# Three joined edits: half rows' pv over 128 keys, slot exponentials transposed in whole blocks, five rows' copies on ScalarE

## The chip, the cores and the metric
The kernel runs on one core of a Trainium2 chip. A core has a TensorE (PE), a VectorE (DVE), a ScalarE (ACT), a GpSimd (POOL) and a SyncE (SP) that issues most DMAs. Each engine works through its own queue in order, and semaphores tie the queues together. The metric is device time in microseconds; a median of three runs stands for a kernel.

## The reference
Three stages follow each other, all in float32 at the outside:

```python
# 4 batches, 8 heads, 576 positions, head dimension 64
scores = q @ k.T / sqrt(64)                       # per head
cum = cumsum(log(clip(f, 1e-4, 1)))
scores = where(causal, -1e9, scores + cum[:, None] - cum[None, :])
x = softmax(scores) @ v                           # -> 2304 tokens x 512

h = x @ w_in                                      # 512 x 2048
x = (h * sigmoid(1.702 * h)) @ w_out              # 2048 x 512

logits = x @ phi                                  # 32 slots, 8 experts x 4
d = softmax(logits, over tokens)                  # slot_input = d.T @ x
slot_out[e] = relu(slot_input[e] @ w1[e]) @ w2[e]
out = softmax(logits, over slots) @ slot_out
```

## The kernel before
A batch has 576 positions, so it falls into four query rows of 128 positions and one of 64. There are 20 such rows r, and each holds all 8 heads. Row 4, 9, 14 and 19 are the half rows. float32 products are made from pairs of f16 values, a high part and the rest.

`prep_row(r)` readies one row. k and q arrive by DMA as f32 (kf and qf; for rows 0 to 2 one tile kqf). ScalarE writes their f16 high parts (L318 kbn, L321 qbn). VectorE copies these into two more tiles (L322 kan, L328 qan), adds three columns of the decay sums (L323, from cpart), and subtracts to get the low parts (L325, L329; GpSimd does this in rows 1 to 4). kan, kbn, qan and qbn are single tiles, used again for every row. They are then transposed: by TensorE and a copy out of PSUM in rows 0 to 2 (L340, L342, L344), by a DMA afterwards (L346).

Rows 0 to 4 find the maximum of each query before the exponentials: score products (L382) and a reduction on VectorE (L387), then L432, a transpose mT (L436) and a ScalarE write into qa (L445), after which the real scores can be made (L467, L469) and the exponential taken (L489). From row 5 on the maximum comes with the score itself (L551, L552, L574), the probabilities are written in two f16 parts (L586, L587) and a DMA transposes them (ph<-pn, L591).

`emit_pv(r, h)` multiplies the probabilities with v, one key block j of 128 positions after another. In rows 5 to 19 each block takes three matmuls, high by high, high by low, low by high (L628 to L630). A half row's last block has 64 keys, and there the operands are sliced to 64 rows. The v tile `vv` has 128 rows; for a half row only 64 of them are filled. The probabilities of a half row's last block are padded with zeros to 128 before the DMA transposes them (L585).

The second stage is `moe_steps`: h = x @ w_in (L800 to L802), the gate (L813, L814), transposes gT (L756) and the product with phi folded into w_out (L778). Its weights arrive as f32 words and are unpacked in the first 165 us by ScalarE, VectorE and GpSimd (L208 to L216, L277, L278; L243 to L269 fold phi). `slot_steps` follows each pair of token blocks: logits lT, the exponential dT over 128 rows (the 32 slots four times), its transposes d (L896), a copy dd (L898), and the slot sums sp (L921).

The order on each engine is made by a scheduler that lays out the recorded instructions by a time model; attention steps and second-stage steps are recorded interleaved, by costs in `attn_items`. The expert weights of the third stage are loaded into tiles that attention leaves, once it has ended.

Of the kernel before, what the change touches and what calls it, by code (L numbers as in the profile page):

```python
# [14 lines left out]
AF = mybir.ActivationFunctionType  # L15
# [15 lines left out]
def attention_moe_softmoe(ctx, tc, q, k, v, f, w_in, w_out, phi, w1, w2, out):  # L31
    nc = tc.nc
    P_PV, P_XT, P_MG, P_W, P_MG2 = (1.2, 2.4, 3000, 5, 8000)
    B, H, S, D = q.shape
    NT, DM = out.shape
    DFF = w_in.shape[1]
    NS = phi.shape[1]
# [21 lines left out]
    kan, kbn, qan, qbn = [ap_.tile([128, H, 128], F16, name=n) for n in ("kan", "kbn", "qan", "qbn")]  # L59
# [14 lines left out]
    ident = const.tile([128, 128], F32, name="ident")  # L74
# [8 lines left out]
    cpart = ap_.tile([128, NQ, BH, 3], F16, name="cpart")  # L83
# [203 lines left out]
    KA, KB, QA, QB, VV = {}, {}, {}, {}, {}  # L287
# [25 lines left out]
    def prep_row(r):  # L313
        b, i = rows[r]
        n = rows_of[i]
        kf, qf = nat.pop((r, "kf")), nat.pop((r, "qf"))
        vf = nat.pop((r, "vf"), None)
        first = nc.scalar.activation(out=kbn[0:n, :, 0:D], in_=kf[0:n], func=AF.Copy)  # L318
        if r == 0:
            tc.keep_in_program_order(first)  # L320
        nc.scalar.activation(out=qbn[0:n, :, D:2 * D], in_=qf[0:n], func=AF.Copy)  # L321
        nc.vector.tensor_copy(kan[0:n, :, 0:D], kbn[0:n, :, 0:D])  # L322
        nc.vector.tensor_copy(kan[0:n, :, D:D + 3], cpart[0:n, i, b * H:(b + 1) * H, :])  # L323
        eng = nc.gpsimd if 1 <= r < 5 else nc.vector
        eng.tensor_tensor(  # L325
            out=kbn[0:n, :, D:2 * D], in0=kf[0:n], in1=kbn[0:n, :, 0:D], op=ALU.subtract
        )
        nc.vector.tensor_copy(qan[0:n, :, 0:D], qbn[0:n, :, D:2 * D])  # L328
        eng.tensor_tensor(  # L329
            out=qbn[0:n, :, 0:D], in0=qf[0:n], in1=qbn[0:n, :, D:2 * D], op=ALU.subtract  # L330
        )
        kab = ap_.tile([128, 2, H, 128], F16, tag=f"kab{r % 6}", name="kab")
        order = ((kan, KA, 0), (qan, QA, "qa"), (kbn, KB, 1), (qbn, QB, "qb"))
        for src, dst, nm in order[::-1] if r < 3 else order:
            t = kab[:, nm] if nm in (0, 1) else ap_.tile([128, H, 128], F16, tag=nm, name=nm, bufs=2)
            if r < 3:

                pt = ps.tile([128, H, 128], F16, tag="mm", name="kqT", bufs=3)
                for h in range(H):
                    nc.tensor.transpose(pt[:, h, 0:n], src[0:n, h, :], ident16[0:n, 0:n])  # L340
                if (nm in (0, 1)) == False:
                    nc.scalar.copy(out=t[:, :, 0:n], in_=pt[:, :, 0:n])  # L342
                else:
                    nc.vector.tensor_copy(t[:, :, 0:n], pt[:, :, 0:n])  # L344
            else:
                nc.sync.dma_start_transpose(  # L346
                    out=t[:, :, 0:n], in_=src[0:n].rearrange("p h c -> p (h c)")
                )
            dst[r] = t
        if b not in B32:  # L350
            vv = ap_.tile([128, 2, H, D + 1], F16, tag="vv", name="vv", bufs=6)
            nc.scalar.activation(out=vv[0:n, 0, :, 0:D], in_=vf[0:n], func=AF.Copy, scale=VS)
            nc.vector.scalar_tensor_tensor(
                out=vv[0:n, 1, :, 0:D], in0=vf[0:n], scalar=VS, in1=vv[0:n, 0, :, 0:D],
                op0=ALU.mult, op1=ALU.subtract,
            )
            nc.gpsimd.memset(vv[0:n, 0, :, D:D + 1], 1.0)
            nc.gpsimd.memset(vv[0:n, 1, :, D:D + 1], 0.0)
            VV[r] = vv
        if r == 0:  # L360
            load_row(0, "v")
            load_row(1, "v")
        elif r + 1 < len(rows):
            load_row(r + 1)
# [245 lines left out]
    def emit_pv(r, h):  # L610
        b, i = rows[r]
        base = ROW[b, 0]
        n = rows_of[i]
        p0 = 64 * (b % 2) if n < 128 else 0
        if h % 4 == 0:
            cur["pv"] = ps_pv("pv")
        pv = cur["pv"].rearrange("p (h c) -> p h c", h=4)
        o = pv[p0:p0 + n, h % 4, 0:D + 1]
        for j in range(i + 1):
            ph, off = PH.pop((r, h, j))  # L620
            rr = rows_of[j]
            if b in B32:
                nc.tensor.matmul(  # L623
                    o, lhsT=ph[0:rr, off:off + n], rhs=VV[base + j][0:rr, h, :], start=(j == 0), stop=(j == i)
                )
                continue
            vh, vl = VV[base + j][0:rr, 0, h, :], VV[base + j][0:rr, 1, h, :]
            nc.tensor.matmul(o, lhsT=ph[0:rr, 0, off:off + n], rhs=vh, start=(j == 0), stop=False)  # L628
            nc.tensor.matmul(o, lhsT=ph[0:rr, 0, off:off + n], rhs=vl, start=False, stop=False)  # L629
            nc.tensor.matmul(o, lhsT=ph[0:rr, 1, off:off + n], rhs=vh, start=False, stop=(j == i))  # L630
        if h % 4 == 3:
            blk = blk_of[r]
            if blk not in XB:
                XB[blk] = ap_.tile([128, DM], F32, tag="x" if n == 128 else "xs", name="x", bufs=1)
            x = XB[blk]
            rd = ap_.tile([128, 4, 1], F32, tag="rd", name="rd", bufs=2)
            nc.vector.tensor_scalar(
                out=rd[p0:p0 + n], in0=pv[p0:p0 + n, :, D:D + 1], scalar1=1e-9 * PB / (VS if b in B32 else 1.0), scalar2=None, op0=ALU.add
            )
            nc.vector.reciprocal(out=rd[p0:p0 + n], in_=rd[p0:p0 + n])  # L640
            g = (h // 4) * 4 * D
            nc.vector.tensor_tensor(
                out=x[p0:p0 + n, g:g + 4 * D].rearrange("p (h d) -> p h d", h=4),
                in0=pv[p0:p0 + n, :, 0:D], in1=rd[p0:p0 + n].to_broadcast([n, 4, D]), op=ALU.mult,
            )
# [4 lines left out]
    for pair in range(B // 2):  # L650
# [4 lines left out]
        n = rows_of[-1]  # L655
# [184 lines left out]
    def slot_steps(c, ts=(0, 1)):  # L840
        fresh = c == 0
        nt = len(ts)
# [3 lines left out]
            out=l4, in0=P4.pop((c, ts[0]))[:, 0:128 * nt], scalar1=1.0 / (GS * WS), scalar2=None, op0=ALU.mult  # L846
# [32 lines left out]
        dT = mp.tile([128, 256], F32, tag="dT", name="dT", bufs=1)[:, 0:128 * nt]  # L879
# [13 lines left out]
        pd = ps_mm("d")  # L893
        with nullcontext() if end else tc.issue_after(last_hp[0].ins):
            for i in range(nt):
                nc.tensor.transpose(pd[:, NS * i:NS * (i + 1)], dT[0:NS, 128 * i:128 * (i + 1)], ident[0:NS, 0:NS])  # L896
        dd = mp.tile([128, 2 * NS], F32, tag="dd", name="dd", bufs=1)[:, 0:nt * NS]
        nc.vector.tensor_copy(dd, pd[:, 0:nt * NS])  # L898
        yield

        if end:
# [8 lines left out]
            for n, v in enumerate(halves):  # L910
                nc.vector.scalar_tensor_tensor(
                    out=spart[:, v], in0=spart[:, v], scalar=nm[:, 1:2], in1=sp[n][:, v], op0=ALU.mult, op1=ALU.add
# [151 lines left out]
    if True:  # L1064
# [26 lines left out]
        n = 0  # L1091
# [10 lines left out]
        for c in range(NCH):  # L1102
            t0, t1 = goals[c], goals[c + 1]
            NSTEP = 2 * N_UNIT
            n = 0
# [181 lines left out]
```

## Time and profile before
| | |
|---|---|
| median of 3 runs | 561.03 us (560.23 to 561.23) |
| profiled execution | 562.1 us, span of its instructions 560.4 us |
| mean granted TensorE clock | 0.973 |
| TensorE busy | 506.8 us (90%), 5387 matmuls |
| VectorE busy | 354.5 us (63%) |
| ScalarE busy | 309.2 us (55%) |
| GpSimd busy | 69.0 us (12%) |
| chain that ended last | PE 70%, DMA 12%, DVE 8%, ACT 5% |

A busy share is a mean over stages with different limits. In the 40 slices of the page TensorE stands at 3 to 6 tenths in the first four (56 us) and at 8 or 9 tenths in nearly all later ones, while GpSimd is busy only in the first nine. A matmul's duration in the profile is the time it takes from start to end; matmuls overlap, so what one costs a full TensorE is read from the starts of neighbours.

### The profile page before, as it was taken

Reading aid. Unit: us, or ns where it says so; the run is one execution under the profiler, and the core shown is the slowest. Engines: PE = TensorE matmul, PEld = TensorE weight load, DVE = VectorE, ACT = ScalarE, POOL = GpSimd, SP = SyncE. Lnnn points to the kernel's source line nnn. Section 1 sums busy time; section 2 is a strip of 40 time slices with the busy share of each in tenths; the row PEclk is TensorE's granted clock in tenths of the full one; section 3 lists DMA queues with packets and bytes.
Section 4 is the critical chain, followed back from the end, with each engine's and each line's share of the span. In section 5 each row is a group of like instructions: output and inputs, shape, how many; then the busy total and the mean of one; then the engine's idle time right before and its main releaser. Section 6 shows DMA issues by size and latency. Waiting matters only on the chain.

```text
span 560.4 us, 13652 instructions
## 1 busy us (share of the span) xinstructions
PE 506.8 (90%) x5387; PEld 317.4 (57%) x5387; DVE 354.5 (63%) x934; ACT 309.2 (55%) x604; POOL 69.0 (12%) x120
## 2 busy tenths in 40 slices
PE   3566999998989999999999799989999999899991
PEld 3455876775666555665665466546566545454431
DVE  8988969787667357577776667866764413352022
ACT  6767786786767354565666566756564233312111
POOL 4866743310000000000000000000000000000000
PEclk9879799998999999999999899999999999999997
DMA  9997674999867227996759979995544199999999
GB/s 241 275 363 173 171 126 151 262 183 190 153 130 121 58 39 146 181 182 99 130 99 151 154 139 155 208 163 104 85 78 79 37 344 369 363 341 338 379 294 284
DMA packets 229823, 105.63 MB, mean 188 GB/s; under 512 B 202592, under 2 KB 211296, under 8 KB 229760
## 3 DMA queue, kind: packets, MB, share of 16 engines
q1 hardware_dynamic: 228528, 103.59, 80.0%
q10 hardware_dynamic: 1232, 1.18, 0.7%
q8 instruction: 42, 0.69, 0.5%
q14 instruction: 21, 0.17, 0.1%
HBM read 64.63 MB, written 4.72 MB: 124 GB/s over the span
## 4 chain that ended last, share of the span: by engine, by line
PE 70%; DMA 12%; DVE 8%; ACT 5%; issue 2%; SPq 2%; ACTq 0%; DVEq 0%
PE hp L800 10%; PE hp L801 9%; PE hp L802 9%; DMA ph<-pn 6%; PE gT L756 5%; PE p L778 4%; PE pv L623 3%; PE pv L628 3%; PE l L1172 3%; PE sp L921 2%; DMA kf<-in_k_dram 2%; PE scs L551 2%; DMA we<-in_moe_w_dram 2%; PE scs L552 2%; PE pv L630 2%
## 5 line engine op out<-in xcount | busy, mean ns | idle before, releaser
L800 PE MATMUL hp<-w,xt 128*128 128x512 f16 x288 | 110.4, 383 | 0.3 <-DVE spart L928 0.3
L801 PE MATMUL hp<-w,xt 128*128 128x512 f16 x288 | 109.8, 381 | 0.0
L802 PE MATMUL hp<-w,xt 128*128 128x512 f16 x288 | 109.7, 381 | 0.0
L578 ACT ACTIVATE pf<-scs,mx 128x512 f32<-128x512 f32 (+3 forms) x108 | 57.6, 541 | 40.9 <-DVE mx L574 31.7
L814 DVE SCALAR_TENSOR_TENSOR g<-g,hp 128x512 f32<-128x512 f32 x72 | 49.2, 683 | 41.6 <-ACT g L813 40.9
L813 ACT ACTIVATE g<-hp 128x512 f32<-128x512 f32 x72 | 42.6, 591 | 51.6 <-PE hp L802 46.4
L587 DVE SCALAR_TENSOR_TENSOR pn<-pf,pn 128x512 f16<-128x512 f32 (+2 forms) x78 | 51.0, 657 | 31.0 <-ACT pn L586 30.4
L586 ACT ACTIVATE pn<-pf 128x512 f16<-128x512 f32 (+2 forms) x78 | 47.0, 606 | 26.3 <-DMA ph<-pn 25.0
L628 PE MATMUL pv<-vv,ph 128*128 128x65 f16 (+2 forms) x360 | 45.9, 199 | 7.9 <-DMA ph<-pn 7.7
L574 DVE CUSTOM_DVE_ANT_0 scs<-scs,zmq 128x128 f32<-128x128 f32 (+3 forms) x96 | 46.6, 495 | 9.1 <-PE scs L552 6.9
L802 PEld LDWEIGHTS <-xt 128*128 128x128 f16 x288 | 28.3, 98 | 33.3 <-issue 0.6
L763 ACT COPY gt<-gT 128x512 f32<-128x512 f32 x71 | 41.1, 583 | 9.7 <-PE gT L756 9.3
L628 PEld LDWEIGHTS <-ph 128*128 128x128 f16 (+2 forms) x360 | 34.4, 102 | 20.0 <-DMA ph<-pn 10.2
L629 PE MATMUL pv<-vv,ph 128*128 128x65 f16 (+2 forms) x360 | 45.3, 196 | 0.0
L756 PE MATMUL gT<-ident,g 128*128 128x128 f32 x288 | 45.1, 277 | 0.0
L630 PE MATMUL pv<-vv,ph 128*128 128x65 f16 (+2 forms) x360 | 45.1, 195 | 0.0
L800 PEld LDWEIGHTS <-xt 128*128 128x128 f16 x288 | 28.8, 100 | 27.8 <-issue 4.7
L756 PEld LDWEIGHTS gT<-ident,g 128*128 128x128 f32 x288 | 33.9, 142 | 14.4 <-issue 5.0
L801 PEld LDWEIGHTS <-xt 128*128 128x128 f16 x288 | 28.3, 98 | 22.7 <-issue 0.7
L629 PEld LDWEIGHTS <-ph 128*128 128x128 f16 (+2 forms) x360 | 34.7, 103 | 1.9 <-issue 0.2
L551 PE MATMUL scs<-kab,qa 128*128 128x128 f16 x240 | 35.2, 220 | 0.4 <-ACT pf L578 0.4
L585 POOL MEMSET pn<- 128x128 f16 x12 | 2.5, 210 | 267.3 <-DMA ph<-pn 165.8
(226 smaller groups left out, 1036.3 us busy)
## 6 DMA issues: line engine op xcount, KB each, us to landing
we<-in_moe_w_dram SPq DMA_DIRECT2D x127, 256.0 KB, 5.6
raw<-in_moe_w_in_dram SPq DMA_DIRECT2D x16, 512.0 KB, 7.3
raw<-in_moe_w_out_dram SPq DMA_DIRECT2D x16, 512.0 KB, 6.0
kf<-in_k_dram SPq DMA_DIRECT2D x13, 256.0 KB, 3.7
qf<-in_q_dram SPq DMA_DIRECT2D x13, 256.0 KB, 4.1
vf<-in_v_dram SPq DMA_DIRECT2D x12, 256.0 KB, 4.4
out_dram<-ob SPq DMA_DIRECT2D x12, 256.0 KB, 3.2
ph<-pn SPq DMA_TRANSPOSE x78, 3.3
```

The source lines that it names most:

```text
L574: nc.vector.tensor_tensor_reduce(out=o, in0=o, in1=mask, scale=-SC, scalar=3.0e38 if n == 128 else DG[r][1][:, u], op0=ALU.add, op1=ALU.mi ...
L578: nc.scalar.activation(out=pf[:, hh * nb:(hh + 1) * nb], in_=o, func=AF.Exp, bias=mx[:, hh:hh + 1], scale=-1.0)
L586: nc.scalar.activation(out=pn[:, 0, 0:w], in_=pf, func=AF.Copy, scale=PB)
L587: nc.vector.scalar_tensor_tensor(out=pn[:, 1, 0:w], in0=pf, scalar=PB, in1=pn[:, 0, 0:w], op0=ALU.mult, op1=ALU.subtract)
L628: nc.tensor.matmul(o, lhsT=ph[0:rr, 0, off:off + n], rhs=vh, start=(j == 0), stop=False)
L629: nc.tensor.matmul(o, lhsT=ph[0:rr, 0, off:off + n], rhs=vl, start=False, stop=False)
L630: nc.tensor.matmul(o, lhsT=ph[0:rr, 1, off:off + n], rhs=vh, start=False, stop=(j == i))
L756: last_turn[0] = nc.tensor.transpose((pt if a < 2 else pt2)[:, a * 128:(a + 1) * 128], g[:, a * 128:(a + 1) * 128], ident)
L800: nc.tensor.matmul(hp, lhsT=xt[:, 0, kk, ts], rhs=win(0, fg, kk), start=(kk == 0), stop=False)
L801: nc.tensor.matmul(hp, lhsT=xt[:, 0, kk, ts], rhs=win(1, fg, kk), start=False, stop=False)
L802: last_hp[0] = nc.tensor.matmul(hp, lhsT=xt[:, 1, kk, ts], rhs=win(0, fg, kk), start=False, stop=(kk == KD - 1))
L814: nc.vector.scalar_tensor_tensor(out=g, in0=g, scalar=1.0, in1=hp, op0=ALU.add, op1=ALU.mult)
```

## The change
Three edits are joined.

1. In `emit_pv` the last key block of a half row is read over all 128 rows, as the other blocks are. The empty 64 rows of the half row's v tile are filled with zeros by GpSimd in `prep_row`. This concerns rows 9, 14 and 19; row 4 takes another branch and stays.
2. In `slot_steps` a transpose of dT reads all 128 rows and writes 128 columns, where it read 32 rows and wrote 32. The copy dd picks the 32 columns of each block that are used.
3. In `prep_row`, for rows 0 to 4, the copies into kan and qan are made by ScalarE from the f32 tiles kf and qf, and the decay columns are copied by ScalarE too. Rows 5 to 19 are as before.

```diff
--- before.py
+++ after.py
@@ -319,13 +319,21 @@
         if r == 0:
             tc.keep_in_program_order(first)
         nc.scalar.activation(out=qbn[0:n, :, D:2 * D], in_=qf[0:n], func=AF.Copy)
-        nc.vector.tensor_copy(kan[0:n, :, 0:D], kbn[0:n, :, 0:D])
-        nc.vector.tensor_copy(kan[0:n, :, D:D + 3], cpart[0:n, i, b * H:(b + 1) * H, :])
+        if r < 5:
+            nc.scalar.activation(out=kan[0:n, :, 0:D], in_=kf[0:n], func=AF.Copy)
+        else:
+            nc.vector.tensor_copy(kan[0:n, :, 0:D], kbn[0:n, :, 0:D])
+        (nc.scalar.copy if r < 5 else nc.vector.tensor_copy)(
+            kan[0:n, :, D:D + 3], cpart[0:n, i, b * H:(b + 1) * H, :]
+        )
         eng = nc.gpsimd if 1 <= r < 5 else nc.vector
         eng.tensor_tensor(
             out=kbn[0:n, :, D:2 * D], in0=kf[0:n], in1=kbn[0:n, :, 0:D], op=ALU.subtract
         )
-        nc.vector.tensor_copy(qan[0:n, :, 0:D], qbn[0:n, :, D:2 * D])
+        if r < 5:
+            nc.scalar.activation(out=qan[0:n, :, 0:D], in_=qf[0:n], func=AF.Copy)
+        else:
+            nc.vector.tensor_copy(qan[0:n, :, 0:D], qbn[0:n, :, D:2 * D])
         eng.tensor_tensor(
             out=qbn[0:n, :, 0:D], in0=qf[0:n], in1=qbn[0:n, :, D:2 * D], op=ALU.subtract
         )
@@ -354,6 +362,8 @@
                 out=vv[0:n, 1, :, 0:D], in0=vf[0:n], scalar=VS, in1=vv[0:n, 0, :, 0:D],
                 op0=ALU.mult, op1=ALU.subtract,
             )
+            if n < 128:
+                nc.gpsimd.memset(vv[n:], 0.0)
             nc.gpsimd.memset(vv[0:n, 0, :, D:D + 1], 1.0)
             nc.gpsimd.memset(vv[0:n, 1, :, D:D + 1], 0.0)
             VV[r] = vv
@@ -624,7 +634,8 @@
                     o, lhsT=ph[0:rr, off:off + n], rhs=VV[base + j][0:rr, h, :], start=(j == 0), stop=(j == i)
                 )
                 continue
-            vh, vl = VV[base + j][0:rr, 0, h, :], VV[base + j][0:rr, 1, h, :]
+            rr = 128
+            vh, vl = VV[base + j][:, 0, h, :], VV[base + j][:, 1, h, :]
             nc.tensor.matmul(o, lhsT=ph[0:rr, 0, off:off + n], rhs=vh, start=(j == 0), stop=False)
             nc.tensor.matmul(o, lhsT=ph[0:rr, 0, off:off + n], rhs=vl, start=False, stop=False)
             nc.tensor.matmul(o, lhsT=ph[0:rr, 1, off:off + n], rhs=vh, start=False, stop=(j == i))
@@ -893,9 +904,11 @@
         pd = ps_mm("d")
         with nullcontext() if end else tc.issue_after(last_hp[0].ins):
             for i in range(nt):
-                nc.tensor.transpose(pd[:, NS * i:NS * (i + 1)], dT[0:NS, 128 * i:128 * (i + 1)], ident[0:NS, 0:NS])
+                nc.tensor.transpose(pd[:, 128 * i:128 * (i + 1)], dT[:, 128 * i:128 * (i + 1)], ident)
         dd = mp.tile([128, 2 * NS], F32, tag="dd", name="dd", bufs=1)[:, 0:nt * NS]
-        nc.vector.tensor_copy(dd, pd[:, 0:nt * NS])
+        nc.vector.tensor_copy(
+            dd.rearrange("p (t s) -> p t s", t=nt), pd[:, 0:128 * nt].rearrange("p (t s) -> p t s", t=nt)[:, :, 0:NS]
+        )
         yield
 
         if end:
```

The scheduler lays the instructions out anew. Line numbers in the pieces of the new order are those of the changed file: L323, L326 and L334 are the copies into kan, its decay columns and qan, L348 to L352 were L340 to L344, L397 was L387.

ScalarE at the start of the program: Ln over f (fs), the table load for Exp, row 0's high parts, row 0's first copy out of PSUM (qb), row 1's high parts. Before:

```order
L140 ACTIVATE fs<-fs 32x576
L142 ACT_TABLE_LOAD
L142 ACTIVATE cres<-fs 32x1
L318 ACTIVATE kbn<-kqf 128x8x64
L321 ACTIVATE qbn<-kqf 128x8x64
L342 COPY qb<-kqT 128x1024
L321 ACTIVATE qbn<-kqf 128x8x64
L318 ACTIVATE kbn<-kqf 128x8x64
L342 COPY qa<-kqT 128x1024
```

Now:

```order
L140 ACTIVATE fs<-fs 32x576
L323 ACTIVATE kan<-kqf 128x8x64
L142 ACT_TABLE_LOAD
L142 ACTIVATE cres<-fs 32x1
L318 ACTIVATE kbn<-kqf 128x8x64
L321 ACTIVATE qbn<-kqf 128x8x64
L334 ACTIVATE qan<-kqf 128x8x64
L350 COPY qb<-kqT 128x1024
L321 ACTIVATE qbn<-kqf 128x8x64
L326 COPY kan<-cpart 128x8x3
L318 ACTIVATE kbn<-kqf 128x8x64
L350 COPY qa<-kqT 128x1024
```

Row 0's copy into kan stands ahead of the table load, its copy into qan behind the high parts, and the decay columns between row 1's high parts.

VectorE between row 1's attention output x and row 2's maxima (mt), with row 2's copies out of PSUM (kab). Before:

```order
L642 TENSOR_TENSOR x<-pv,rd 128x256
L344 COPY kab<-kqT 128x1024
L328 COPY qan<-qbn 128x8x64
L344 COPY kab<-kqT 128x1024
L322 COPY kan<-kbn 128x8x64
L323 COPY kan<-cpart 128x8x3
L387 TENSOR_REDUCE mt_83<-scm 128x1 x5
L675 TENSOR_TENSOR xt<-xT,xt 128x4x128
```

Now:

```order
L653 TENSOR_TENSOR x<-pv,rd 128x256
L352 COPY kab<-kqT 128x1024 x2
L397 TENSOR_REDUCE mt_83<-scm 128x1 x6
L686 TENSOR_TENSOR xt<-xT,xt 128x4x128
```

Row 3's three copies are gone from between the last copy out of PSUM and the first maximum.

TensorE after row 1's maxima (mT): the first pv of row 0, then row 1's scores (scs) before, the transposes of row 2 (kqT) now. Before:

```order
L436 MATMUL mT<-ident,mt_84 104x128
L623 MATMUL pv<-vv,pf 128x65 x4
L467 LDWEIGHTS kab
L467 MATMUL scs<-qa,kab 128x128
L469 LDWEIGHTS kab
```

Now:

```order
L446 MATMUL mT<-ident,mt_84 104x128
L633 MATMUL pv<-vv,pf 128x65 x4
L348 LDWEIGHTS qbn
L348 MATMUL kqT<-ident_76,qbn 128x128
L348 LDWEIGHTS qbn
```

The transposes of qbn, kbn and qan of row 2, 24 in all, now stand ahead of row 1's scores.

## Rows read from the trace of the kernel before

**Rows 1.** Stretches: length; busy PE, PEld, DVE, ACT, POOL; PE clock, DMA share, GB/s.
```profile
0.00:60.00 60.00, 33.65 (x346) 30.51 (x347) 53.51 (x99) 41.46 (x66) 40.07 (x57) 0.88 0.93 248
340.00:450.00 110.00, 107.50 (x1191) 64.89 (x1189) 71.74 (x211) 62.49 (x127) 1.28 (x12) 1.00 0.65 115
```

**Rows 2.** TensorE's waits: for whom, us in total, times, longest.
```profile
PE pv L628 <- DMA ph<-pn: 7.7, 9, 2.0
PE mT L436 <- DVE mt L432: 7.5, 2, 6.9
PE scs L467 <- DVE mt L387: 6.9, 2, 5.5
```

**Rows 3.** Timeline of TensorE, half row 9: start, us, line, out<-in, rows*columns.
```profile
234.11 0.19 PE L629 MATMUL pv<-vv,ph 128*64 128x65 f16 x1
234.14 0.20 PE L630 MATMUL pv<-vv,ph 128*64 128x65 f16 x1
234.26 0.21 PE L628 MATMUL pv<-vv,ph 64*64 64x65 f16 x1
...
234.47 0.22 PE L628 MATMUL pv<-vv,ph 128*64 128x65 f16 x1
...
235.06 0.19 PE L630 MATMUL pv<-vv,ph 64*64 64x65 f16 x1
235.18 0.23 PE L552 MATMUL scs<-kab,qb 128*128 128x128 f16 x1
```

**Rows 4.** Groups by form, L628: count, busy us, mean ns, idle before.
```profile
L628 PE MATMUL pv<-vv,ph 128*64 128x65 f16 x96 | 12.1, 202 | 1.0 <-DMA ph<-pn 1.0
...
L628 PE MATMUL pv<-vv,ph 64*64 64x65 f16 x24 | 5.2, 215 | 0.0
```

**Rows 5.** Timeline of TensorE around one pair of d transposes.
```profile
252.36 0.22 PE L552 MATMUL scs<-kab,qb 128*128 128x128 f16 x1
252.41 0.22 PE L551 MATMUL scs<-kab,qa 128*128 128x128 f16 x1
252.56 0.30 PE L896 MATMUL d<-ident,dT 32*128 32x32 f32 x2
252.80 0.23 PE L552 MATMUL scs<-kab,qb 128*128 128x128 f16 x1
```

**Rows 6.** Timeline of TensorE at four gT transposes.
```profile
226.83 0.60 PE L756 MATMUL gT<-ident,g 128*128 128x128 f32 x4
227.36 0.41 PE L778 MATMUL p<-gt,wphi 128*32 128x128 f32 x5
```

**Rows 7.** VectorE's busy time before 61.5 us: L322, L323, L328.
```profile
0.00:61.50 61.50, 3.41 (x5) 0.87 0.92 244
...
0.00:61.50 61.50, 2.29 (x5) 0.87 0.92 244
...
0.00:61.50 61.50, 5.35 (x5) 0.87 0.92 244
```

**Rows 8.** Timeline of VectorE at rows 3 and 4.
```profile
36.51 0.29 DVE L328 COPY qan<-qbn 128x512 f16<-128x512 f16 x1 [0.33 <-ACT qbn L321]
...
37.89 1.20 DVE L322 COPY kan<-kbn 128x512 f16<-128x512 f16 x1
39.01 1.13 DVE L323 COPY kan<-cpart 128x24 f16<-128x24 f16 x1
...
57.29 3.35 DVE L328 COPY qan<-qbn 64x512 f16<-64x512 f16 x1
```

**Rows 9.** Timeline of GpSimd, first and last of three instructions.
```profile
57.04 1.20 POOL L325 TENSOR_TENSOR kbn<-kf,kbn 64x512 f16<-64x512 f32 x1
...
59.32 1.14 POOL L278 TENSOR_TENSOR w<-w,w 128x512 f16<-128x512 f32 x1
```

**Rows 10.** Timeline of ScalarE at row 0: table load for Exp, kbn.
```profile
4.31 1.28 ACT L142 ACT_TABLE_LOAD   x1
...
5.71 0.61 ACT L318 ACTIVATE kbn<-kqf 128x512 f16<-128x512 f32 x1
```

## The prediction

> **What bounds the kernel now.** I read the busy times by stretch first [rows 1]. In the first 60 us the TensorE is busy for 33.65 us and the VectorE for 53.51, ScalarE for 41.46 and GpSimd for 40.07: three engines that prepare rows and unpack weights hold the TensorE up, and its granted clock is 0.88 there. Between 340 and 450 us it is busy for 107.50 of 110 at clock 1.00, and the stretches between look alike. So an edit before 60 us is worth what it takes off the chain of preparing engines; an edit after that is worth the TensorE time it saves, less what comes back as a wait. The list of TensorE's waits [rows 2] names both kinds: 7.5 us at mT and 6.9 us at the score products L467 for the VectorE, both in the first stage, and 7.7 us in 9 pieces at pv (L628) for the transposed probabilities, which is all that late attention makes it wait for. Last I read the instruction rows where each edit sits [rows 3 to 10].
>
> **Half rows' pv over 128 keys.** The three matmuls of a head's last key block work on 64 rows, all others of that head on 128. They are themselves as long either way: 202 ns on 128 rows, 215 on 64 [rows 4], so the added rows cost nothing on the array. What costs is the change of shape [rows 3]: two matmuls of one shape start 0.03 us apart (234.11, 234.14); from 128 rows to 64 it takes 0.12 (234.14 to 234.26), and out of 64 rows 0.12 again (235.06 to 235.18). From the last 128-row matmul to what follows the block it is 0.33 (234.14 to 234.47), with the next head behind it or, the exits being equal, with another kind of product. Afterwards the three run on at 0.03 to 0.035 each. Where the next head follows, four such steps are 0.13: saved 0.20. Where another shape follows, the exit's 0.12 stays: three steps and it are 0.22, saved 0.12. There are 24 such blocks [rows 4], 3 rows of 8 heads; counted in the order, 9 are followed by the next head and 15 by something else: 9 x 0.20 + 15 x 0.12 = 3.6 us of TensorE time, all after 220 us where it is full. The edit adds three fills on GpSimd (64 partitions x 1040 elements). No row shows that size; a GpSimd subtraction of 512 elements took 1.14 [rows 9], so each is between nothing and 2.3 us. They lie a whole row of scores ahead of the pv that reads them, on an engine busy for 69.0 us of 560, hence nothing; without that cover up to 3 x 2.3.
>
> **Slot exponentials in whole blocks.** Eighteen transposes, eight pairs and two single ones, change from 32 rows and 32 columns to 128 and 128. Before, a pair between score products takes 0.39 from the product ahead of it to the one behind (252.41 to 252.80) [rows 5], where that product alone takes 0.06 (252.36 to 252.41). A 128-column f32 transpose takes 0.11: the four gT run from 226.83 to 227.36, 0.53, of which one change of shape (0.09, that is 0.12 less 0.03) is not theirs [rows 6]. After: 0.06 + 2 x 0.11 = 0.28, saved 0.11. In the new order five pairs stand between full-shape products (0.55); three touch the narrow phi products, where a change of shape stays, and save about 0.02 each; the two single ones stand at the end behind a wait, and I set their longer run against the change saved: nothing. Sum 0.6 us. The copy out of PSUM reads as many elements as before.
>
> **Five rows' copies on ScalarE.** VectorE loses 15 copies, 3.41 + 2.29 + 5.35 = 11.05 us [rows 7]. Left alone such a copy takes 0.29 (36.51), but those that run beside GpSimd took 1.20, 1.13 and 3.35 [rows 8]; the last began at 57.29 and ended at 60.64, just after three GpSimd instructions that ended at 60.46 [rows 9]. ScalarE gains ten copies from f32, 0.61 each by kbn [rows 10], and five of 24 elements, between nothing and 0.61, taken as 0.2: 7.1 us. That is not the sum's term, since neither engine is the path throughout. Along the path:
> (a) Row 0's k copy now stands ahead of the table load for Exp (4.31) and so of kbn (5.71). It adds at least 0.5, and at most 1.9, were k's rows to land only as kbn starts; I take 0.9. The VectorE has two copies of 0.29 less ahead of the split that the first transposes wait for, so they start 0.4 later.
> (b) ScalarE gets six more instructions before it can hand row 0's maxima over, about 2 us. Of that I let 1.4 fall into waits it has anyway (it is idle for 18.5 of the first 60 us), and 0.6 is late. VectorE's unpacking of the weights takes turns with ScalarE, so the wait of 6.9 us at mT near 30 us stays [rows 2] and ends 0.6 later.
> (c) For row 3, kan and cpart (37.89 to 40.14) stand between the last copy out of PSUM and the first maximum of row 2 [rows 8]. Both go, and row 2's transposes are moved ahead of row 1's last scores, so that ScalarE's copy of qa for row 2, which the maxima need, is no longer behind them. The first maximum then comes at about 38 in place of 40.1: 2.0 gained, the 0.6 of (b) taken off.
> (d) Up to the moment when ScalarE passes row 2's maxima on (L445) its own queue has row 3's three copies in it, and its exponentials and weight pieces behind them; 0.6 goes back. 1.4 is left.
> (e) Row 4's 3.35 us copy goes. TensorE does not wait in those microseconds, so I count 0.6.
> Together 2.0 us. Bounds: TensorE's two waits for VectorE add up to 14.4 us [rows 2], of which 6.9 stays by (b), so at best 7.5 is gained; at worst all 7.1 us of ScalarE are on the path and nothing is gained. The nearest row is the stretch of (c), and 2.0 is what is left of it.
>
> The Trainium skill ("ScalarE: Activation LUTs", Rules for kernel authors) speaks against this edit: it leaves simple single-source work to VectorE, which it puts at up to about three times ScalarE's speed in 16 bits. By 0.29 against 0.61 the trace agrees for a copy that nothing disturbs, and by the three disturbed ones it does not; followed alone, the rule makes edit three a loss of at most those 7.1 us, the third rival below. On the disturbance, "SBUF — State Buffer" (its section on the shared port pair) says that whichever of the two engines starts first holds the pair for its whole instruction. The 3.35 us copy outlasted three GpSimd instructions, not one, so here the measurement decides, and a copy taken away frees more than the rule would give.
>
> **Sum.** 3.6 + 0.6 + 2.0 = 6.2 us less. The profiled execution took 562.1 us (span 560.4), 1.1 above the median of 561.03; from the median it comes to 554.8, so 555. The expert weights are loaded once attention has ended and its tiles are free, so these loads move with what is saved earlier, and the last stage with them.
>
> **Rivals.**
> One: the saved TensorE time turns into longer waits for the transposed probabilities, since those come from ScalarE, VectorE and a DMA that are no faster. For it: 7.7 us of such waits exist. Against: they fall in 9 places, and hardly any within the half rows' own stretches, where the array is full. Then only 2.0 is left, 559.
> Two: the early chain gains all of 7.5. For it: the VectorE is busy for 53.5 of 60 us and gets 11 free. Against: its longest stretch, up to 30 us, loses almost no instruction. 549.
> Three, slower: ScalarE becomes the bound of the first 50 us. Its place is the queue of rows 0 to 3, where every copy stands in order ahead of a PSUM copy or an exponential; its price is up to 7.1 us, against 4.2 saved later: 564. It decides once more than 4.2 of the 7.1 is on the path. Against: 18.5 us of idle time there.
> Four: the order between 60 and 180 us, which the scheduler lays differently (scores, weight folding and pv change places), loses about what the edits save, 4 to 6 us: 561.
>
> **How the numbers follow.** Forecast 0.58, with 552 to 558 for its own unknowns ((a), (b), and waits that give part back); rival one 0.14, two 0.10, three 0.10, four 0.08. Faster by over 0.2% (1.1 us, about what a measurement of this kernel tells from nothing): forecast, one and two, 0.82. Within 0.2%: four, 0.08. Slower: three, 0.10. For 8 in 10 the range goes from 549.5, the nearer half of rival two, to 560.8, the better half of four, and leaves out three.
>
> **What would show it.** Half rows: no 64-row matmul at pv, heads 0.03 apart across the block, three late rows shorter by 1.2 us each. Blocks: d pairs without a gap on either side. Early: no DVE copy over 1 us before 60 us but for row 5's; the first maximum of row 2 near 38 us, the first transposes near 9.0; mT's long wait still 6 to 7 us and ending near 31. I am wrong on the early term if TensorE is not dense by 55 to 57, on the half rows if waits for ph grow by 2 us or more, and altogether if TensorE's busy time after 220 us does not fall by about 4.

## The result: slower by 1.4%

The changed kernel takes 571.08 us in the median of 6 runs (569.02 to 572.95), the kernel before 561.19 beside it (560.23 to 562.95). The recorded ratio, with its 95% interval, is 1.0142 [1.0108, 1.0177]; the two medians are 1.8% apart, at the interval's upper end. I had forecast 555, a range up to 560.8, and slower with a chance of 0.10. The profiled execution took 572.95, its span is 571.2.

The stretches of [rows 1], after (length; busy PE, PEld, DVE, ACT, POOL; PE clock, DMA share, GB/s):

```profile
0.00:60.00 60.00, 33.99 (x342) 30.46 (x343) 46.04 (x84) 46.65 (x81) 40.30 (x58) 0.87 0.91 248
340.00:450.00 110.00, 104.60 (x1173) 63.74 (x1172) 73.62 (x219) 64.02 (x133) 2.56 (x14) 0.97 0.69 116
```

The copies did move: 7.5 us less VectorE, 5.2 more ScalarE in the first 60 us. TensorE did as much there as before, and between 340 and 450 us it is busy for 2.9 us less, so it waits for longer, and its granted clock is lower, 0.97 in place of 1.00. Its waits, as in [rows 2]:

```profile
PE pv L639 <- DMA ph<-pn: 8.8, 9, 2.6
PE mT L446 <- DVE mt L442: 7.6, 2, 7.0
PE scs L477 <- DVE mt L397: 6.5, 1, 6.5
...
PE scs L561 <- ACT pf L588: 2.1, 2, 1.8
...
PE wps L269 <- ACT part L258: 1.8, 1, 1.8
```

The two long early waits stand as predicted for mT and unlike predicted for L477, and two on ScalarE are new or longer (L561, L269). These two lie between 124 and 190 us. That stretch, first before, then after:

```profile
124.00:190.00 66.00, 61.72 (x702) 40.62 (x702) 43.59 (x127) 43.72 (x89) 0.75 (x10) 0.97 0.81 140
```

```profile
124.00:190.00 66.00, 58.78 (x653) 38.29 (x654) 44.06 (x131) 44.58 (x92) 0.00 (x0) 0.95 0.86 148
```

Of the edits' instructions that TensorE runs only the first pair of d transposes sits there; the first five rows are long prepared. What did change is the order of TensorE's products.

What the edits themselves do to an instruction came out as worked out. A half row's pv, row 9, at its end, as in [rows 3]:

```profile
239.93 0.20 PE L639 MATMUL pv<-vv,ph 128*64 128x65 f16 x1
239.96 0.20 PE L640 MATMUL pv<-vv,ph 128*64 128x65 f16 x1
239.99 0.20 PE L641 MATMUL pv<-vv,ph 128*64 128x65 f16 x1
240.12 0.23 PE L562 MATMUL scs<-kab,qb 128*128 128x128 f16 x1
```

and a pair of d transposes, as in [rows 5]:

```profile
257.01 0.22 PE L561 MATMUL scs<-kab,qa 128*128 128x128 f16 x1
257.07 0.39 PE L907 MATMUL d<-ident,dT 128*128 128x128 f32 x2
257.29 0.22 PE L562 MATMUL scs<-kab,qb 128*128 128x128 f16 x1
```

No change of shape within the heads, 0.03 from product to product, one exit of 0.13; and the pair takes 0.28 (257.01 to 257.29), as predicted.

### The profile page after: what moved, and what is told of

Its sections match the earlier page's. It is cut to its first block, busy times and chain, and to the rows that moved or that the text cites. A ratio compares the mean times of both kernels' runs of the same rounds, so it can differ in the third digit from the quotient of the medians.

```text
span 571.2 us, 13651 instructions
## 1 busy us (share of the span) xinstructions
PE 510.9 (89%) x5387; PEld 317.7 (56%) x5387; DVE 348.2 (61%) x919; ACT 314.7 (55%) x619; POOL 71.7 (13%) x123
## 4 chain that ended last, share of the span: by engine, by line
PE 57%; DMA 19%; DVE 10%; ACT 6%; issue 3%; SPq 3%; POOL 1%; ACTq 0%; DVEq 0%; POOLq 0%
PE hp L811 8%; PE hp L812 8%; PE hp L813 8%; DMA ph<-pn 7%; PE gT L767 4%; PE pv L633 3%; PE p L789 3%; DMA we<-in_moe_w_dram 3%; DMA kf<-in_k_dram 3%; PE l L1185 3%; PE sp L934 2%; PE pv L639 2%; DMA kab<-kan 2%; PE kqT L348 2%; PE scs L561 2%
## 5 line engine op out<-in xcount | busy, mean ns | idle before, releaser
L811 PE MATMUL hp<-w,xt 128*128 128x512 f16 x288 | 112.2, 389 | 0.8 <-ACT gt L774 0.3
L812 PE MATMUL hp<-w,xt 128*128 128x512 f16 x288 | 111.8, 388 | 0.0
L813 PE MATMUL hp<-w,xt 128*128 128x512 f16 x288 | 111.4, 387 | 0.0
L639 PE MATMUL pv<-vv,ph 128*128 128x65 f16 (+1 forms) x360 | 42.4, 197 | 10.4 <-DMA ph<-pn 8.8
L584 DVE CUSTOM_DVE_ANT_0 scs<-scs,zmq 128x256 f32<-128x256 f32 (+3 forms) x96 | 46.7, 497 | 6.9 <-PE scs L562 4.5
L813 PEld LDWEIGHTS <-xt 128*128 128x128 f16 x288 | 28.8, 100 | 34.2 <-issue 2.7
L639 PEld LDWEIGHTS <-ph 128*128 128x128 f16 (+1 forms) x360 | 33.9, 102 | 22.0 <-DMA ph<-pn 12.9
L811 PEld LDWEIGHTS <-xt 128*128 128x128 f16 x288 | 29.4, 102 | 28.6 <-issue 6.7
L812 PEld LDWEIGHTS <-xt 128*128 128x128 f16 x288 | 28.7, 100 | 24.2 <-issue 3.1
L641 PE MATMUL pv<-vv,ph 128*128 128x65 f16 (+1 forms) x360 | 41.9, 194 | 0.0
L640 PE MATMUL pv<-vv,ph 128*128 128x65 f16 (+1 forms) x360 | 41.9, 195 | 0.0
L561 PE MATMUL scs<-kab,qa 128*128 128x128 f16 x240 | 35.2, 220 | 2.8 <-ACT pf L588 2.1
L641 PEld LDWEIGHTS <-ph 128*128 128x128 f16 (+1 forms) x360 | 34.4, 103 | 1.4 <-issue 1.0
```

Of the source, the lines that this page charges most:

```text
L561: nc.tensor.matmul(o, lhsT=QA[r][:, h, :], rhs=KA[base + j][:, h, :], start=True, stop=False)
L584: nc.vector.tensor_tensor_reduce(out=o, in0=o, in1=mask, scale=-SC, scalar=3.0e38 if n == 128 else DG[r][1][:, u], op0=ALU.add, op1=ALU.mi ...
L811: nc.tensor.matmul(hp, lhsT=xt[:, 0, kk, ts], rhs=win(0, fg, kk), start=(kk == 0), stop=False)
L812: nc.tensor.matmul(hp, lhsT=xt[:, 0, kk, ts], rhs=win(1, fg, kk), start=False, stop=False)
L813: last_hp[0] = nc.tensor.matmul(hp, lhsT=xt[:, 1, kk, ts], rhs=win(0, fg, kk), start=False, stop=(kk == KD - 1))
```

## The experiments

Theory one: the scheduler's new order of TensorE is what costs, whatever the edits do. Theory two: ScalarE's 7 us of added copies cost it. To see where a run loses, I add up TensorE's products along its order, each at the usual distance to the next in the run of before, and note how much later than before each run reaches the same sum ("lateness", in us, at the time of before in the head). It is good to about half a microsecond; in the new order the column of 120 is good to about 1.5 only, since it shifts with how the usual distance is taken. "Old order" is TensorE's order of before, "new" that of the copies' edit alone. The run of before is one execution, 1.1 us above its kernel's median.

| run, TensorE's order | 50 | 80 | 120 | 190 | 270 | 330 | 350 | 400 | 450 |
|---|---|---|---|---|---|---|---|---|---|
| changed kernel, its own | -0.6 | 1.7 | 0.8 | 6.8 | 5.8 | 6.7 | 5.5 | 11.5 | 10.1 |
| e16, the same again | -1.2 | -0.8 | -0.9 | 5.5 | 4.5 | 2.8 | 1.6 | 3.6 | 2.2 |
| e1 copies, new | -0.8 | -0.7 | 1.4 | 8.6 | 8.0 | 8.6 | 8.6 | 8.1 | 8.1 |
| e5 copies, old | 0.1 | 1.5 | 1.6 | 1.6 | 1.3 | -1.1 | -1.1 | -1.4 | -1.4 |
| e6 no edit, new | 1.2 | 3.8 | 3.3 | 12.8 | 12.3 | 9.7 | 9.7 | 10.4 | 10.4 |
| e2 half rows, old | 0.0 | 0.0 | -0.2 | -0.6 | -1.6 | -1.1 | -2.3 | 0.6 | -0.7 |
| e3 blocks, own | 0.9 | 2.0 | 2.0 | 2.0 | 1.4 | 0.0 | 0.0 | 0.1 | -0.1 |
| e7 all three, old | 0.0 | 2.2 | 3.4 | 2.2 | 1.3 | -1.0 | -2.1 | 0.1 | -1.1 |
| e9 no edit, new from 124 us | 0.0 | -0.1 | -0.2 | 2.8 | 2.8 | 2.1 | 2.1 | 3.1 | 3.1 |
| e10 no edit, new up to 124 us | 0.0 | 1.4 | 1.2 | 14.9 | 14.5 | 13.3 | 13.3 | 13.2 | 13.2 |
| e15 no edit, new, covered | -1.1 | -1.2 | -1.4 | 6.6 | 6.0 | 3.6 | 3.6 | 5.1 | 5.1 |

### One edit at a time: e1, e2, e3, e4

Each takes single pieces of the diff: e1 edit 3, e2 edit 1, e3 edit 2, e4 edits 1 and 2. In the orders as laid out, edit 3 alone shifts TensorE's products between the 143rd and the 1615th of 4556, edit 2 some between the 1385th and the end, edit 1 none. (The profile counts 5387: a float32 product, other than a transpose, stands in it twice.) The changed kernel has both shifts.

> Only the five rows' copies go to ScalarE. This edit alone gives the TensorE the changed kernel's order between 46 and 190 us, and leaves the order after 220 us as before. Theory one, the new order: about 6 to 7 us slower than before (567 to 568), the loss built up between 46 and 190 us where ScalarE's ten copies have long been done. Theory two, ScalarE is the bound: also slower, but the loss stands whole by 50 us, with ScalarE busy without a break there. Theory three, the half rows' fills or the slot blocks cost it: faster than before by up to 2 us (559).

> Only the half rows' products over 128 keys, with the three fills. No engine's order changes but for the fills. If my term of 24 blocks is right: 3.6 us faster, between 2.5 and 4 (557 to 558.5). If the saved time only turns into waits for the transposed probabilities: within 1 us of before, and pv's waits for the DMA of ph grow by 2 to 3 us. If the fills cost: slower.

> Only the slot exponentials' transposes in whole blocks. The TensorE's order changes with it in stretches between 190 and 400 us. Theory one, the order: 4 to 5 us slower (565 to 566), lost between 375 and 400 us, as in the changed kernel. If the transposes were all there is to it: 0.6 faster (560.4).

> Half rows and slot blocks, no copies on ScalarE. If the edits add up: the sum of the two runs before it, about 1 us slower than the kernel before by theory one (562); 4.2 faster (556.8) by the sum of my prediction's two terms.

Measured, as ratios to before with their 95% intervals: e1 1.0123 [1.0077, 1.0168]; e2 0.9964 [0.9933, 0.9994]; e3 1.0000 [0.9977, 1.0024]; e4 0.9976 [0.9946, 1.0006]. So the copies' edit brings most of the loss, and it brings it after ScalarE's copies are done: e1 is 0.8 us ahead at 50 us and 8.6 behind at 190. e3 missed: the 4 to 5 us that I expected from its order near 375 to 400 us are not there. e2 is 2.0 us faster (0.3 to 3.8), between its two expectations; its interval just holds the 3.6 of my term. e4's, at most 3.0 us faster, leaves out the 4.2 of my two terms.

### Order against edit: e5, e6, e7, e8

The order is held by edges from each product to the one before it on TensorE; they make nothing wait for another engine. e5 is e1 so held to the old order, e6 is the kernel before held to e1's order, e7 and e8 are the changed kernel and e4 held to the old order.

```diff
+def pin_order(tc, nc):
+    mm = [i for i in nc.cur_bb.bb.instructions if i.engine == mybir.EngineType.PE]
...
+        for ins in mm[int(first):int(first) + int(count or 1)]:
+            if last is not None:
+                tc.add_manual_dep(
+                    ins, last.name,
+                    mybir.DependencyInfo(mybir.DependencyClass.NoSync, mybir.DependencyReason.DATA),
...
```

With TensorE's order the scheduler lays out the other engines' too. Against before about 100 of ScalarE's 604 instructions and 140 of VectorE's some 900 stand elsewhere in e6, and fewer than ten of each in e5, not counting the copies that moved. So "order" means from here on what all three engines run once TensorE's is held; no run parts them.

> The copies on ScalarE as in the run with this edit alone, but TensorE's 4556 matmuls and transposes are held in the order of the kernel before by order edges without waits; the other engines' orders follow it but for the moved copies. Theory one (the order loses it): the loss of 7 us goes, and what is left is the edit's own gain, 0 to 2 us faster than before (560 to 562.5). Theory two (ScalarE's extra 7 us lose it, whatever the order): 5 to 7 us slower (568 to 570).

> No edit at all, but TensorE held in the order that the copies' edit gave it (46 to 190 us). Theory one: 6 to 9 us slower than before (569 to 571), since the order alone does it. Theory two: no change (562.5).

> All three edits with TensorE held in the order of the kernel before. Theory one: the sum of the edits without the order, at best my predicted 6.2 us faster, by the single runs 2 to 4 faster (558.5 to 560.5), and the PE work lost between 380 and 396 us in the changed kernel shrinks to the 1.6 of the half rows alone. Theory two: about 5 us slower than before (567).

> Half rows and slot blocks with TensorE held in the order of the kernel before, copies as before. If the slot blocks are worth their 0.6 us when no order changes: 0.6 less than the half rows alone, about 2.5 us faster than before (560). If half rows' gain is lost in waits for the transposed probabilities at 344 and 384 us whatever the order: 1 to 2 us faster (561 to 561.5).

| | old order | new order |
|---|---|---|
| no edit | 1 | e6 1.0192 [1.0165, 1.0220] |
| copies on ScalarE | e5 1.0025 [1.0006, 1.0044] | e1 1.0123 [1.0077, 1.0168] |

e7 0.9994 [0.9970, 1.0019], e8 0.9983 [0.9954, 1.0011].

Theory two falls: the copies in the old order cost at most 0.44%, and the order costs 1.9% with no edit at all. But the two do not add up. With the copies in, the order costs 1.0% (e1 beside e5, 5.5 us), with all three edits 1.5% (the changed kernel beside e7, 8.3 us); and in the new order, which was laid out for copies on ScalarE, the kernel with the copies is the faster one (e1 beside e6). The stretch shows the order's loss too, e5, then e6:

```profile
124.00:190.00 66.00, 61.60 (x706) 40.21 (x706) 44.41 (x128) 44.04 (x90) 0.75 (x10) 0.97 0.83 142
```

```profile
124.00:190.00 66.00, 54.44 (x616) 36.78 (x613) 41.27 (x128) 42.63 (x89) 0.70 (x10) 0.97 0.88 144
```

TensorE is busy for 61.60 with the edit in the old order (before 61.72) and for 54.44 without it in the new one, at one granted clock, 0.97: the difference is waiting. e7 says the second thing: even with the order kept, the three edits together give 0.06%, not my 1.1%, nor the 2 to 4 us that I expected of e7. e8 gives 0.17%, where I expected 1 to 2.5 us.

What TensorE waits for in e6 is ScalarE and VectorE. Its rows where the folding of w_out begins (a start, its duration, the idle time ahead and what ended it):

```profile
130.87 0.66 PE L243 MATMUL woT<-ident,wo 128*128 128x128 f32 x4 [0.56 <-DVE g L814]
131.45 0.43 PE L253 MATMUL wq<-woT,phi_sb 128*32 128x128 f32 x8
133.67 0.63 PE L269 MATMUL wps<-rsum,part 128*128 128x32 f32 x4 [1.79 <-ACT part L258]
```

and ScalarE's queue over the same time:

```profile
130.81 0.66 ACT L586 ACTIVATE pn<-pf 128x512 f16<-128x512 f32 x1
131.34 0.64 ACT L321 ACTIVATE qbn<-qf 128x512 f16<-128x512 f32 x1
131.86 0.64 ACT L352 ACTIVATE vv<-vf 128x512 f16<-128x512 f32 x1
132.38 0.49 ACT L578 ACTIVATE pf<-scs,mx 128x256 f32<-128x256 f32 x1
132.74 0.61 ACT L245 COPY woT<-woT 128x512 f32<-128x512 f32 x1
133.20 0.41 ACT L258 COPY part<-wq 128x256 f32<-128x256 f32 x1
```

The new order puts the step that needs part right behind the product that makes wq, where ScalarE, which works in order, has a row's preparation (qbn, vv) and two more instructions ahead of the copy into part (L258). In before the copy of part follows closely, and 14 score products stand in the gap:

```profile
125.69 0.43 PE L253 MATMUL wq<-woT,phi_sb 128*32 128x128 f32 x8
126.84 0.58 PE L269 MATMUL wps<-rsum,part 128*128 128x32 f32 x4
```

### Where the order loses: e9, e10, e15

e9 and e10 join the two orders at TensorE's 860th product, about 124 us. e15 is e6 with 23 score products put back between L253 and L269.

> No edit; TensorE in the order of before for its first 860 products (to about 124 us), then the rest as the copies' edit had put it. If the loss is where the weight folding, the rows' pv and the scores are laid anew after 124 us: 5 to 9 us slower than before. If the first 124 us made it: within 2 us of before.

> No edit; TensorE's first 860 products in the order that the copies' edit gave them, the rest in the order of before. If the loss is made after 124 us: 0 to 4 us slower than before. If the first 124 us made it: 8 to 11 slower. The two runs together should come to the 11 us of the whole new order if each part has its own loss.

> No edit, the copies' new order, but 23 score products (1.3 us) that it puts ahead of the two weight foldings near 128 to 133 us stand, as in the order of before, between a folding's product and the step that waits for ScalarE's copy of it. If such uncovered waits are how the order loses time: that 2.1 us wait shrinks to under 1, and the time falls by about 1 us from the new order's (1.7 in place of 1.9% slower). If the wait is ScalarE's backlog whatever covers it: it stays at 2 us.

Measured: e9 1.0063 [1.0034, 1.0093]; e10 1.0258 [1.0216, 1.0301]; e15 1.0137 [1.0081, 1.0193]. The halves do not add up to the whole (0.6 + 2.6 against 1.9%), and e10 is worse than the whole new order though it has the good order after 124 us: it is 1.2 late at 120 us and 14.9 at 190. So no stretch of TensorE's order is good or bad by itself. The likely reason is that what is queued on the other engines when it is reached decides, and that this comes from the order ahead of it: in e10 the longest waits between 120 and 190 us are 4.0 for ph and 3.5 for ScalarE's gt, where before has none over 2.2. No run changes those queues alone. A part of e10's loss is not waiting, but the clock after the waits:

```profile
124.00:190.00 66.00, 53.21 (x553) 36.11 (x552) 38.69 (x114) 41.03 (x83) 0.00 (x0) 0.87 0.83 140
```

A granted clock of 0.87 in place of 0.97 over 66 us is 6.6 us of the full clock. Both of my expectations for e10 (0 to 4 us, 8 to 11 us) missed its 14.5, and e9's 3.5 lies between the two for it.

e15's waits on TensorE, 124 to 170 us (us in total, times, longest):

```profile
PE pv L628 <- DMA ph<-pn: 3.8, 2, 3.1
PE woT L243 <- DVE g L814: 2.1, 1, 2.1
...
PE wps L269 <- ACT part L258: 0.2, 1, 0.2
```

The covered wait is gone (1.8 to 0.2, as expected), and the time falls by half a per cent from e6's, more than the 0.2 that I expected, though the intervals overlap. But a wait of 3.1 for ph has come, and with it a stretch at the lower clock:

```profile
142.00:148.00 6.00, 5.98 (x27) 3.15 (x28) 1.96 (x8) 1.16 (x3) 0.00 (x0) 0.50 0.91 174
```

At 0.50 these 6 us cost 3.0 of the full clock. e15 still loses 8 us from 120 to 190: covering one wait moved part of the loss on.

### A tiny edit, and fills moved by hand: e11, e12

e11 moves only the five copies of 24 elements. e12 is e2 with six groups of products moved ahead of waits for ph.

```diff
-        nc.vector.tensor_copy(kan[0:n, :, D:D + 3], cpart[0:n, i, b * H:(b + 1) * H, :])
+        (nc.scalar.copy if r < 5 else nc.vector.tensor_copy)(kan[0:n, :, D:D + 3], cpart[0:n, i, b * H:(b + 1) * H, :])
```

> Only the five copies of 24 elements a partition (cpart into kan) go to ScalarE, about 1 us of work in all; the 512-element copies stay on VectorE. TensorE's order between 46 and 190 us comes out anew all the same, and unlike both others. If a new order is what costs: several us slower than before (563 to 571), though 1 us of work moved. If what costs is the work on ScalarE: within 1 us of before.

> Half rows' edit in the order of before, but at six places where TensorE waits for the transposed probabilities (near 309, 317, 349, 372, 377 and 392 us, 0.9 to 2.6 us each, some 8 us in all in the run of the half rows alone) independent products that stand just behind the wait (expert products, scores) are put ahead of it, 0.6 to 1.7 us each. If the order sets what the half rows are worth: 3 to 7 us faster than the half rows alone (554 to 558). If the probabilities' chain is the bound there and not TensorE's order: no faster than the half rows alone (559).

e11: 1.0038 [1.0011, 1.0066], 2.1 us slower for about 1 us of work that moved: a third order, a third time. It lies below the several microseconds that I expected, and can't be told from the cost of the work itself. e12: 1.0019 [0.9993, 1.0046], no faster than e2; my order was no better. Waits for ph between 300 and 400 us fell from 8.0 (e2) to 3.8, and the time came back as waits on other chains:

```profile
PE pv L631 <- DMA ph<-pn: 3.8, 6, 1.2
PE pv L631 <- DVE x L645: 2.0, 2, 1.5
PE gT L759 <- ACT gt L766: 1.2, 1, 1.2
PE scs L553 <- DVE xt L678: 1.0, 1, 1.0
```

That points to the chain of scores, exponentials and transposes as what sets the pace in that stretch, and not to where TensorE's fills stand; one order tried by hand does not prove it.

### The second loss, 350 to 400 us: e13, e14, e16

The changed kernel's profile loses another 6.0 us there (5.5 to 11.5). e13 has edits 3 and 1, e14 has 3 and 2, e16 is the changed kernel once more, in a single run.

> Copies on ScalarE and half rows, slot blocks as before; TensorE's order as in the run of the copies alone (46 to 190 us), after 220 us as before. If the 4 to 5 us that the changed kernel loses between 375 and 396 us come from the half rows' earlier arrival at waits for the transposed probabilities: they appear here too, about 569 to 571 (1.3% slower). If they need the slot blocks' order of 310 to 396 us: they don't, and this comes to the copies alone less 2 (about 567, 0.9% slower).

> Copies on ScalarE and slot blocks, half rows as before; TensorE's order is the changed kernel's throughout. If the loss between 375 and 396 us comes from the order of 310 to 396 us: it is here, 570 to 572 (1.6% slower). If it needs the half rows: it is not, and this comes to the copies alone, 568 to 569 (1.2%).

> The changed kernel as it is, for a second profiled execution. If its loss between 370 and 396 us belongs to the three edits together: TensorE again waits over 2 us for the transposed probabilities near 387 us and falls 3 to 5 us further behind the kernel before there. If it was that execution's own: it loses under 2 us there, as the runs of two edits do, and stands 6 to 8 us behind at the end.

e13 1.0097 [1.0059, 1.0135], e14 1.0141 [1.0102, 1.0180]; they lose 1.4 (4.6 to 6.0) and 1.6 us (4.8 to 6.4) there. e16 took 564.97 beside 562.33 for the kernel before, and loses 2.0 (1.6 to 3.6). So 2 us of that loss recur and 4 were that one execution's. Most of the 4 are the clock. The stretch in the changed kernel, then in e16:

```profile
350.00:400.00 50.00, 45.08 (x424) 25.53 (x424) 34.47 (x97) 29.84 (x59) 1.53 (x9) 0.93 0.84 147
```

```profile
350.00:400.00 50.00, 45.79 (x489) 27.89 (x488) 35.96 (x107) 31.82 (x66) 0.00 (x0) 1.00 0.87 145
```

After its wait of 2.6 us for ph, which ends at 387.23, the changed kernel's granted clock falls; over the 50 us it is 0.93 in place of 1.00 (before has 1.00 too), and 0.07 of 50 us is 3.5. e16's longest wait there is 1.5. The 2 us are not the half rows' alone: e14, without them, and e15, with no edit, lose 1.6 and 1.5 there. e13's interval holds both of its expectations, and e16 missed one half of its own: it ends 2.2 us behind, not 6 to 8. What else makes the changed kernel differ by up to 8 us between executions (564.97 to 572.95) is not settled. That e16 also loses 6.4 us from 120 to 190 recurs: every run in the whole new order loses 6.0 to 9.5 us there by the table's measure (1.5 less if the column of 120 is off by that), and no run in the old order more than 0.5.

## Why the prediction was wrong, step by step

- **The step that failed: the sum had no term for the order, and rival four, which was the case, had too small a price.** I named the order between 60 and 180 us, priced it at 4 to 6 us by what the edits save, and gave it 0.08. With the three edits in, the order costs 8.3 us (the changed kernel beside e7); with none, 10.8 (e6). The price had no row under it. I had shown three places where the order changes, costed only these, and left the rest at nothing. **And the 6.2 us that the edits were to save came to 0.3 (e7),** so even rival four's balance, loss against saving, did not hold. The next points say where the 6.2 went.
- **Early term, (a) and (b): right.** In the changed kernel the first transposes start at 8.81 (predicted 9.0), and mT's long wait of 7.0 us stays and ends at 31.0 (predicted 31). In e16 it is 5.0 and ends at 30.4.
- **Early term, (c): right in kind, about half its size.** The first maximum of row 2, predicted at about 38 in place of 40.1, in the kernel before and in the changed one:

```profile
40.04 2.13 DVE L387 TENSOR_REDUCE mt<-scm 128x1 f32<-128x384 f32 x4
```

```profile
38.93 1.49 DVE L397 TENSOR_REDUCE mt<-scm 128x1 f32<-128x384 f32 x3 [0.36 <-PE scm L394]
```

  That is 1.1 earlier, where I had 2.0.
- **Early term, (d) and (e): wrong.** Of the 1.4 to be left, 0.6 to 1.2 is there at 50 us in the runs with the copies in a new order (the table), 0.1 is lost with the old order (e5), and next to none is left at 57: the longest wait for row 3's maxima grows from 5.5 [rows 2] to 6.5 and ends at 56.91, before at 56.46. These maxima stand in VectorE's queue behind the unpacking of weights, pairs of L213 and L216 that take turns with ScalarE and GpSimd. In e5:

```profile
53.27 1.55 DVE L213 SCALAR_TENSOR_TENSOR low<-w,low 128x512 uint32<-128x512 uint32 x1
54.73 0.41 DVE L650 TENSOR_TENSOR x<-pv,rd 128x256 f32<-128x256 f32 x1
55.07 1.63 DVE L216 SCALAR_TENSOR_TENSOR w<-w,low 128x512 uint32<-128x512 uint32 x1
56.63 1.27 DVE L395 TENSOR_REDUCE mt<-scm 128x1 f32<-128x512 f32 x2
```

  An unpacking step that takes 0.68 at 52.58 takes 1.6 here. In before one of this last group is slow too (1.31 at 54.43), so it looks as if the slowing that I had seen on the copies now falls on others; no run shows the cause. Taking copies off VectorE did not shorten this chain, and the term is 0, not 2.0. The 0.6 of (e) had no row under it: I had said myself that TensorE does not wait there.
- **Half rows: the saving right, the claim that no wait takes it wrong in the trace.** In e2, whose order is that of before, the three late rows gain 1.0 (190 to 270 us), 1.2 (330 to 350) and 1.3 (from 0.6 late at 420 to 0.7 ahead at 450): 3.5 against my 3.6; the three fills take 0.96 each in the changed kernel, and nothing waits for them. From 350 to 400 us 2.9 is given back, at pv:

```profile
370.62 0.20 PE L631 MATMUL pv<-vv,ph 128*128 128x65 f16 x1 [0.74 <-DMA ph<-pn]
371.88 0.20 PE L631 MATMUL pv<-vv,ph 128*128 128x65 f16 x1 [0.72 <-DMA ph<-pn]
377.25 0.20 PE L631 MATMUL pv<-vv,ph 128*128 128x65 f16 x1 [1.17 <-DMA ph<-pn]
391.79 0.20 PE L631 MATMUL pv<-vv,ph 128*128 128x65 f16 x1 [1.36 <-DMA ph<-pn]
```

  The last is new (before, that product waits for nothing); 0.88 at 348.92 for VectorE's x is new too, and these two are 2.2 of the 2.9. Over the whole run e2's waits for ph, 7.7 in before [rows 2], are

```profile
PE pv L631 <- DMA ph<-pn: 10.1, 10, 2.5
```

  and a growth of 2 us or more was my sign of being wrong. This is rival one. I had set it aside because hardly any of these waits lies within the half rows' own stretches; they lie in the row behind. In the times it shows with the slot blocks added: in the old order half rows and blocks gain 2.6 us at most (e8), not 4.2.
- **Slot blocks: right between full-shape products, and too small to see.** Four pairs take 0.28 as worked out. Two beside the narrow phi products went from 0.44 to 0.48, where I had 0.02 saved. e3 is unchanged within 0.24%.
- **Rival three: wrong.** ScalarE is not the bound (e5). The rule that I weighed from the Trainium skill ("ScalarE: Activation LUTs", Rules for kernel authors) points the right way: in the old order the copies on ScalarE lose 0.06 to 0.44%, 0.3 to 2.5 us of the 7.1 that the rule would have cost at most. In the new order the kernel with the copies on ScalarE is the faster one (e1 beside e6).

Of both kernels and all the runs, the half rows alone are the fastest: 0.9964 [0.9933, 0.9994] of before.

## What to carry to other kernels

Where a scheduler lays out the order, an edit has two effects, its own and that of the order it draws; compare the orders first, and if one engine's order changes over a long dense stretch, give that a term of its own. Here new orders cost from nothing (e3) to 14.5 us (e10), and none gained. Holding the critical engine's order while the edit goes in tells the two apart, in both directions (edit without order, order without edit); what the order costs still depends on the edit it is run with. TensorE time that is saved is gained only up to the next wait for another chain, which may be in the row behind.

## What the runs showed of the chip that I had not expected

After the wait of 5.4 to 5.6 us that ends near 57 us TensorE's granted clock is at its lower level, 1.2 GHz, and how long it stays there differs between executions with one and the same TensorE order (e3's is that of before up to 183 us). The stretch from 56 to 64 us in before, in e2 and in e3:

```profile
56.00:64.00 8.00, 7.54 (x48) 6.45 (x48) 7.93 (x9) 5.43 (x11) 7.14 (x6) 0.60 0.61 85
```

```profile
56.00:64.00 8.00, 7.54 (x57) 6.06 (x57) 7.93 (x9) 5.51 (x12) 7.16 (x6) 0.76 0.60 116
```

```profile
56.00:64.00 8.00, 6.78 (x43) 6.21 (x43) 7.88 (x9) 6.18 (x12) 7.22 (x6) 0.50 0.51 80
```

At 0.50 the whole 8 us run at half the full clock. e3 is 0.9 late at 50 us and 2.0 at 80, e2 on time at both. Later it turns round: around the waits for ph near 309 to 317 us the clock falls in before and stays in e3, the stretch from 304 to 328 us of before and of e3:

```profile
304.00:328.00 24.00, 20.48 (x265) 12.59 (x263) 15.77 (x37) 14.62 (x27) 0.41 (x2) 0.93 0.77 127
```

```profile
304.00:328.00 24.00, 20.30 (x268) 12.64 (x267) 16.12 (x37) 14.77 (x27) 0.45 (x2) 1.00 0.85 133
```

A mean of 0.93 over 24 us is 1.7 us of the full clock, and e3 is 1.4 late at 270 us and on time at 330. Here e3's order is its own, but e5, in the old order, has 1.00 there too. So one profile's lateness of 2 us may be the clock's, in either direction, and terms of 1 or 2 us in one stage are read from a stretch at full clock or from several runs.
